# One accumulating bank for both expert groups, output and product in pieces, and a moved weight load, in a fused attention and mixture-of-experts kernel

## Chip, cores and metric

The kernel runs on one core of a Trainium2 chip. The metric is the device time of one execution in microseconds. "The span" is the time from the first to the last instruction in the profiled execution.

## What is computed

Three steps follow one another on 4 x 768 = 3072 tokens of 384 features, all in float32:

```python
x = attn(q, k, v, a_re, a_im)      # scan over time, 32 heads of 48, complex decay
logits = x @ phi                   # 32 slots, 4 for each of 8 experts
d = softmax over tokens (logits);  slot_input = d.T @ x          # 32 x 384
for e in range(8):                 # 4 slots each
    h = maximum(slot_input[e] @ w1[e], 0.0)    # 384 -> 1024
    slot_out[e] = h @ w2[e]                    # 1024 -> 384
x = softmax over slots (logits) @ slot_out     # 3072 x 384
h = x @ w_in;  out = maximum(0.01 * h, h) @ w_out   # 384 -> 2048 -> 384
```

The kernel multiplies slot_out with w_in first (32 slots x 2048, "product"), and only then with the 3072 rows of combine weights.

## The kernel before

A planner (`Plan`, lines 97 to 296) holds every operation with an engine, an estimated cost, what it reads and writes, and a `lead` that raises its priority. It lays all operations out in time by these estimates and then emits them in that order, so each engine's queue is a fixed order. `after` gives the planner an order between two operations and nothing else. Tiles come from tags with a fixed number of buffers; waits follow from the tiles that an instruction touches.

The stages, in order of time: attention in 12 units with the slot sums of `slots`; the experts; the feed-forward part.

*Experts.* The weights w1 and w2 are 64 slabs of 128 x 768 (384 KB): 32 of w1, 32 of w2. `load_slabs` (line 406) issues them on SP through `load` (line 351; all loads carry line 352). Some w2 slabs lie in pairs of half-size buffers (`halved`). The experts are two groups of four; expert g of a group uses column group g of TensorE, 32 output partitions from 32g on. All 32 slots are multiplied with each expert's weights, and the 4 right ones are cut out afterwards.
`layer1(gr)` (line 924) runs once for each group: four steps i of 12 matmuls (L934, two instructions each) into two banks, then ReLU on ACT (L939) or DVE (L941), transposes (L945) and copies of each expert's slots (L952) into h1T, which holds zeros elsewhere. `layer2(gr)` (line 958) adds 32 matmuls (L970) into a bank of its own for each group. `output(gr)` (line 978) scales 384 columns by 1/den on ACT (L982), transposes three blocks (L986) and copies the slots of four experts on DVE (L994) into soT.
siT holds the slot inputs, transposed; DVE writes it (L915).

*Product* (line 1002): for each half j of w_in's columns, 12 matmuls (L1014), a high part on ACT (L1017) and a low part on DVE (L1018), then four selections g, each of two matmuls (L1022, L1023) into bank g, copied to gs by ACT (even g, L1029) or DVE (odd g, L1027).

*Feed-forward.* `ffn1` (line 1036) makes one 128 x 384 block of h for step f and row block j: a matmul (L1039), leaky ReLU on ACT (L1041), its high part on ACT (L1042), its low part on DVE (L1043). `ffn2` adds three matmuls for each row tile (L1056 to L1058). The first double loop runs 16 steps f over j = 0 and 1 and needs w_out of step f as a high and a low part. `conv_wo` (line 465) makes these from 64-bit words: a load, Abs on ACT (L439), four operations on DVE (L440 to L443), a copy on ACT (L471), a subtraction on DVE (L472). Step 0 of these has a lead of 26; the others have none.

`combine_t` makes transposed combine weights; its last copies (L884) read banks of the pool `psa`, whose space the expert stage's banks (`psb`) take over.

*Start.* `load_a` (line 482) loads a_re on SP and a_im of unit 0 on ACT's queue; unit 0 comes in three cuts.

Of the kernel before, what the change touches and what calls it, by code (L numbers as in the profile page):

```python
# [10 lines left out]
F32 = mybir.dt.float32  # L11
# [8 lines left out]
DM = H * D  # L20
# [299 lines left out]
def tile_kernel(  # L320
# [63 lines left out]
    t_dd = Tag(mem, "dd", [P, P], 3)  # L384
# [19 lines left out]
    stream = iter([(l, gr, i, g) for l in range(2) for gr in range(2) for i in range(4) for g in range(4)])  # L404

    def load_slabs(n, homes=None):

        for _ in range(n):
            key = next(stream, None)
            if key is None:  # L410
                return
# [7 lines left out]
            for j, (k, v) in enumerate(slabs[key]):  # L419
                n = W // len(slabs[key])  # L420
                load(k, v, src[:, n * j:n * j + n], P * n * 4)
# [59 lines left out]

    def load_a(u):
        s = st[u]
        for i, nm in enumerate(("re", "im")):
            b = s[nm] = t_w()
            for o, e in cuts(u):
                far = u == 0 and i
                plan.add("ACT" if far else "SP", 0.1, lambda b=b, i=i, o=o, e=e, far=far: (A if far else SY).dma_start(b()[:, o:e], a_in[u, i][:, o:e]), [], [(b, o)], nbytes=P * (e - o) * 4)
# [245 lines left out]
    def slots(c):  # L734
# [4 lines left out]
        b, e, lg = (b_sc if last else b_m)(), t_dd(), t_dd()  # L739
# [21 lines left out]
        b2, dd = (b_sc if last else b_m)(), t_dd()  # L761
# [133 lines left out]
    rd, siT, wb = t_sm([P, 1]), t_dd([P, 3, NSL]), t_kt([P, 4, NSL])  # L895
    dg, mt = t_kt([P, P]), t_sm()
    m = nm[:, NCH:NCH + 1]
    b2 = b_sc()
# [16 lines left out]
    si = dve(0.17, lambda: V.tensor_copy(siT().rearrange("p k s -> p (k s)"), b1()[:, :3 * NSL]), [(b1, k) for k in range(3)], [siT])  # L915
# [6 lines left out]
    pool(0.6, lambda: GP.memset(h1T().rearrange("p k s r g i -> p (k s r g i)"), 0.0), [], [(h1T, r, j, g) for r in range(2) for j in range(2) for g in range(4)])  # L922

    def layer1(gr):
        hb = [bank() for _ in range(2)]
        for i in range(4):
            sl = [slabs[0, gr, i, g][0] for g in range(4)]
            assert all(len(slabs[0, gr, i, g]) == 1 for g in range(4))

            def mm(i=i, sl=sl):  # L930
                for k in range(3):
                    for g in range(4):
                        o = 256 * (i % 2)
# [233 lines left out]
```

## Time and profile before

| | us |
|---|---|
| median of 3 runs | 501.98 (501.07 to 503.56) |
| profiled execution, its own time | 502.35 |
| its span | 500.6 |
| granted TensorE clock, mean | 1.000 |
| busy: TensorE matmul / weight load | 485.2 / 440.0 |
| busy: ScalarE / VectorE / GpSimd | 356.5 / 318.6 / 18.2 |

PE is TensorE's matmul, PEld its weight load, ACT ScalarE, DVE VectorE, POOL GpSimd, SP the engine that issues most loads. Line numbers (L970) are those of the kernel before. Rows give a start and a duration from the start of the span.

### The profile page before, as it was taken

The numbers are of one execution on the slowest core, as the hardware profiler recorded it, in microseconds if no ns is written. First come the engines' busy times: TensorE is split into PE (matmuls) and PEld (weight loads), VectorE is DVE, ScalarE is ACT, GpSimd is POOL, SyncE is SP. The second block draws the span as 40 slices with busy tenths as digits, with TensorE's granted clock in tenths as the row PEclk, the third lists the DMA queues.
The fourth block names the chain that finished last, engine by engine and source line by source line (L and its number), as shares of the span: only waits on it lengthen the run. The fifth ranks groups of instructions, "written<-read, shape, count | busy, mean of one in ns | idle before, by whom it ended". The sixth has DMA issues, their size and how long they took to land.

```text
span 500.6 us, 10447 instructions
## 1 busy us (share of the span) xinstructions
PE 485.2 (97%) x4066; PEld 440.0 (88%) x4066; DVE 318.6 (64%) x669; ACT 356.5 (71%) x684; POOL 18.2 (4%) x37
## 2 busy tenths in 40 slices
PE   8797999999999999999999999999999999999997
PEld 8675779979979988889545999999999999999996
DVE  3767899999999998986535999334500542035300
ACT  7998999999999999944215998079802993079502
POOL 1010002001001000001000000000000000000000
PEclk9999999999999999999999999999999999999999
DMA  8987344465677393599899221011000010010002
GB/s 300 324 196 234 98 129 147 109 192 142 181 221 217 75 260 118 191 323 318 286 395 352 64 64 33 0 48 48 2 0 33 17 48 1 0 48 16 33 1 94
DMA packets 46890, 67.09 MB, mean 134 GB/s; under 512 B 22004, under 2 KB 28132, under 8 KB 46840
## 3 DMA queue, kind: packets, MB, share of 16 engines
q1 hardware_dynamic: 46088, 65.99, 41.4%
q8 instruction: 32, 0.52, 0.4%
q10 hardware_dynamic: 432, 0.39, 0.2%
q0 software_dynamic: 320, 0.03, 0.1%
q14 instruction: 18, 0.15, 0.1%
HBM read 61.59 MB, written 4.81 MB: 133 GB/s over the span
## 4 chain that ended last, share of the span: by engine, by line
PE 70%; DVE 15%; ACT 8%; DMA 5%; issue 1%; SPq 0%; ACTq 0%; DVEq 0%
PE b L1056 13%; PE b L1058 13%; PE b L1057 13%; PE bm L683 5%; PE bsc L658 5%; PE b L1039 4%; PE btr L643 4%; PE bc L562 3%; PE bsc L700 3%; DMA w<-in_w_dram 2%; DVE w L619 2%; DVE sc L661 2%; DMA w<-in_wo_dram 2%; DVE q L628 2%; DVE k L628 1%; PE b L934 1%
## 5 line engine op out<-in xcount | busy, mean ns | idle before, releaser
L1043 DVE TENSOR_TENSOR w<-x,w 128x384 fp32r<-128x384 f32 x128 | 69.0, 555 | 104.6 <-ACT w L1042 103.8
L1056 PE MATMUL b<-w 128*128 128x384 f32 x384 | 128.5, 335 | 0.0
L1058 PE MATMUL b<-w 128*128 128x384 f32 x384 | 128.3, 334 | 0.0
L1057 PE MATMUL b<-w 128*128 128x384 f32 x384 | 128.3, 334 | 0.0
L1056 PEld LDWEIGHTS b<-w 128*128 128x128 f32 x384 | 72.1, 188 | 0.3 <-ACT x L1041 0.2
L1057 PEld LDWEIGHTS b<-w 128*128 128x128 f32 x384 | 72.1, 188 | 0.0
L1058 PEld LDWEIGHTS b<-w 128*128 128x128 f32 x384 | 72.1, 188 | 0.0
L1065 ACT ACTIVATE k<-b 128x384 f32<-128x384 f32 x24 | 11.4, 488 | 79.1 <-PE b L1058 78.9
L1042 ACT ACTIVATE w<-x 128x384 fp32r<-128x384 f32 x128 | 63.4, 525 | 4.9 <-PE b L1058 3.2
L1041 ACT ACTIVATE x<-b 128x384 f32<-128x384 f32 x128 | 59.9, 487 | 2.4 <-PE b L1039 1.5
L658 PE MATMUL bsc<-qt,kt 96*128 96x128 f32 x384 | 50.8, 278 | 0.4 <-DVE S L710 0.2
L658 PEld LDWEIGHTS bsc<-qt,kt 96*128 96x128 f32 x384 | 46.4, 192 | 2.1 <-DVE S L710 0.5
L661 DVE TENSOR_TENSOR sc<-bsc,tri_r 128x512 f32<-128x512 f32 x48 | 32.5, 684 | 7.3 <-PE bsc L658 6.9
L683 PE MATMUL bm<-sc,w 128*64 128x128 f32 (+1 forms) x384 | 35.5, 275 | 0.0
L649 ACT ACTIVATE qt<-btr 96x512 f32<-96x512 f32 x48 | 28.4, 591 | 9.2 <-PE btr L643 9.1
L186 ACT ACT_TABLE_LOAD x25 | 32.1, 1283 | 2.6 <-issue 2.2
L643 PE MATMUL btr<-ident,k 128*96 128x128 f32 x192 | 29.3, 275 | 2.4 <-ACT kt L649 1.7
L683 PE MATMUL bm<-qt,S 96*48 96x128 f32 x320 | 31.1, 272 | 0.0
L700 PEld LDWEIGHTS bsc<-w,k 128*96 128x96 f32 x320 | 28.9, 165 | 2.0 <-issue 1.0
L643 PE MATMUL btr<-ident,q 128*96 128x128 f32 x192 | 29.5, 276 | 1.2 <-DVE kt L647 0.6
L700 PE MATMUL bsc<-w,k 128*96 128x48 f32 x320 | 29.6, 247 | 0.3 <-PE bm L771 0.3
L643 PEld LDWEIGHTS btr<-ident,q 128*96 128x96 f32 x192 | 21.0, 127 | 6.2 <-issue 1.7
(179 smaller groups left out, 798.2 us busy)
## 6 DMA issues: line engine op xcount, KB each, us to landing
w<-in_w_dram SPq DMA_DIRECT2D x50, 384.0 KB, 6.1
w<-in_qkv_dram SPq DMA_DIRECT2D x36, 384.0 KB, 5.9
w<-in_a_dram SPq DMA_DIRECT2D x22, 384.0 KB, 4.2
w<-in_wi_dram SPq DMA_DIRECT2D x16, 384.0 KB, 4.2
w<-in_wo_dram SPq DMA_DIRECT2D x16, 384.0 KB, 5.5
out_dram<-k SPq DMA_DIRECT2D x24, 192.0 KB, 1.9
cs<-in_w_dram SPq DMA_DIRECT2D x4, 384.0 KB
k<-in_w_dram SPq DMA_DIRECT2D x6, 192.0 KB, 3.7
```

The lines of the kernel that those rows point to most:

```text
L186: self.preload(TABLES[name])
L643: T.transpose(b()[:96, P * i:P * i + P], src()[:, i].rearrange("p t d -> p (t d)"), ident)
L658: T.matmul(b()[:, P * i:P * i + P], lhsT=k()[:96, i, :], rhs=q()[:96, i, :], start=True, stop=True)
L661: dve(c_dve(512), lambda: V.tensor_tensor(t(), b().rearrange("p (i t) -> p i t", t=P), tri.unsqueeze(1).to_broadcast([P, 4, P]), op=ALU.mu ...
L683: T.matmul(y()[64 * j:64 * j + m, o:o + P], lhsT=l, rhs=r, start=kind == 0, stop=kind == 1 or c == 0)
L700: T.matmul(b()[:96, D * i:D * i + D], lhsT=ks[i // 4]()[:, i % 4].rearrange("p t d -> p (t d)"), rhs=v()[:, D * g:D * g + D], start=True, ...
L1041: act(NG, lambda: A.activation(u(), b()[:, :NG], AF.Prelu, alpha=0.01), [b], [u])
L1042: act(NG, lambda: A.activation(g()[:, 0], u(), AF.Copy), [u], [(g, 0)])
L1043: dve(c_dve(NG), lambda: V.tensor_tensor(g()[:, 1], u(), g()[:, 0].bitcast(F32), op=ALU.subtract), [u, (g, 0)], [(g, 1)])
L1056: T.matmul(b()[:, :DM], lhsT=lh, rhs=wh()[:, i], start=f == FO[0], stop=False)
L1057: T.matmul(b()[:, :DM], lhsT=ll, rhs=wh()[:, i], start=False, stop=False)
L1058: T.matmul(b()[:, :DM], lhsT=lh, rhs=wl()[:, i], start=False, stop=f == FO[-1])
```

## The change

- The slabs come in the order layer, step, group, expert. `layer1(j)` now covers two steps i of both groups, which add into one bank: siT has 48 columns for each k (16 slots of group 0, 16 zeros, 16 slots of group 1), and each group multiplies with a window of 32, in which the other group's slots are zero. GpSimd clears siT; DVE copies group 0's slots, ACT group 1's. ReLU, transposes and copies run on halves of the bank.
- `layer2()` adds both groups into one bank; `output()` runs once, in three pieces of 128 columns that share the transposes' bank.
- The last four slabs are loaded in halves, the four first halves first, and the last step is split so.
- `product()` waits for one k at a time; the second half has a lead lower by 8; two selections share a bank.
- Step 0 of `conv_wo` loses its lead of 26.
- In the first four units of `ffn1` the high part is written by ACT from the bank.
- In the planned order, unit 1's a_re load comes after unit 0's loads.

```diff
-    stream = iter([(l, gr, i, g) for l in range(2) for gr in range(2) for i in range(4) for g in range(4)])
+    stream = iter([(l, gr, i, g) for l in range(2) for i in range(4) for gr in range(2) for g in range(4)])
...
+        for _, _, k, v, src, n in sorted(later, key=lambda x: x[:2]) if homes is None or together else later:
+            load(k, v, src, P * n * 4)
...
+    def pieces(n):
+
+        out = []
+        for _ in range(n):
+            b = t_w([P, 2, HW])
+            out.append([((b, j), lambda b=b, j=j: b()[:, j]) for j in range(2)])
+        return out
...
+                    [], [(b, o)], nbytes=P * (e - o) * 4, after=[s0[-1]] if u == 1 and not i else [],
...
+    pool(0.3, lambda: GP.memset(siT().rearrange("p k s -> p (k s)"), 0.0), [], [(siT, r) for r in range(2)])
...
-    si = dve(0.17, lambda: V.tensor_copy(siT().rearrange("p k s -> p (k s)"), b1()[:, :3 * NSL]), [(b1, k) for k in range(3)], [siT])
+    own = lambda gr: b1()[:, :3 * NSL].rearrange("p (k r s) -> p k r s", r=2, s=16)[:, :, gr]
+    si = dve(0.15, lambda: V.tensor_copy(siT()[:, :, 0:16], own(0)), [(b1, k) for k in range(3)], [(siT, 0)])
+    act(48, lambda: A.activation(siT()[:, :, 32:48], own(1), AF.Copy), [(b1, k) for k in range(3)], [(siT, 1)])
...
+    def layer1(j):
+        hb = bank()
+        for i in (2 * j, 2 * j + 1):
+            for gr in range(2):
...
+                            T.matmul(
+                                hb()[32 * g:32 * g + 32, o:o + 256], lhsT=siT()[:, k, 16 * gr:16 * gr + NSL],
+                                rhs=sl[g][1]()[:, 256 * k:256 * k + 256], start=k == 0 and gr == 0, stop=k == 2 and gr == 1,
+                            )
+
+                pe(1.3, mm, [(siT, gr)] + [x[0] for x in sl], [hb, (hb, i % 2)])
+        hs, bs = t_kt(), [bank() for _ in range(2)]
+        for n in range(2):
+            x = slice(256 * n, 256 * n + 256)
+            if n:
+                act(256, lambda x=x: A.activation(hs()[:, x], hb()[:, x], AF.Relu), [(hb, n)], [(hs, n)])
+            else:
+                dve(c_dve(256), lambda x=x: V.tensor_scalar(hs()[:, x], hb()[:, x], 0.0, None, op0=ALU.max), [(hb, n)], [(hs, n)])
...
+    def layer2():
+        b = l2[0] = bank()
+        for i in range(4):
+            for gr in range(2):
+                sl = [slabs[1, gr, i, g] for g in range(4)]
+                for js in ((0,), (1,)) if len(sl[0]) > 1 and i == 3 and gr else ((0, 1),):
...
+    def output():
+        b = l2[0]
         plan.lead = 25.0
         so, b2 = t_x(), bank()
...
+        for k in range(3):
+            x = slice(P * k, P * k + P)
+            act(P, lambda x=x: A.activation(so()[:, x], b()[:, x], AF.Copy, scale=rd()), [b, rd], [(so, k)])
+            pe(0.12, lambda k=k, x=x: T.transpose(b2()[:, 160 * k:160 * k + P], so()[:, x], ident), [(so, k)], [(b2, k)])
+            for gr in range(2):
+                own = lambda k=k, gr=gr: b2()[:, 160 * k:160 * k + 144].rearrange("p (g c) -> p g c", c=36)[:, :, 16 * gr:16 * gr + SPE]
+                dve(0.09, lambda k=k, gr=gr, own=own: V.tensor_copy(soT()[:, k, 16 * gr:16 * gr + 16].rearrange("p (g i) -> p g i", i=SPE), own()), [(b2, k)], [(soT, gr, k)])
...
+        N, lead = 256, plan.lead
+        bs, b2 = [bank() for _ in range(2)], {}
         for j in range(2):
             b, y = bs[j], slice(N * j, N * j + N)
+            plan.lead = lead - 8.0 * j
+            for k in range(3):
...
+                pe(0.44, mm, [(soT, r, k) for r in range(2)] + [(wi[2 * g + j], i) for g in range(4) for i in range(2)], [b])
...
+                if g % 2 == 0:
+                    b2[g // 2] = bank()
+                b4, z = b2[g // 2], slice(N * (g % 2), N * (g % 2) + N)
...
+        if j < 2 and f in FO[:ahead]:
+            act(NG, lambda: A.activation(g()[:, 0], b()[:, :NG], AF.Prelu, alpha=0.01), [b], [(g, 0)])
+            act(NG, lambda: A.activation(u(), b()[:, :NG], AF.Prelu, alpha=0.01), [b], [u])
...
-    load_slabs(64)
+    load_slabs(8)
+    load_slabs(4, pieces(4), True)
     select()
...
     for f in FO[:4]:
-        plan.lead = 26.0 if f in FO[:1] else 0.0
+        plan.lead = 0.0
         conv_wo(f)
```

## Rows read from the trace of the kernel before

**Rows 1.** The page, busy time of each engine, share of the span, instructions.
```profile
PE 485.2 (97%) x4066; PEld 440.0 (88%) x4066; DVE 318.6 (64%) x669; ACT 356.5 (71%) x684; POOL 18.2 (4%) x37
```
**Rows 2.** Two stages: length, busy of each engine, clock, DMA share, GB/s.
```profile
249.00:266.00 17.00, 17.00 (x216) 7.57 (x208) 5.21 (x25) 2.28 (x4) 1.04 (x2) 1.00 1.02 392
275.00:287.00 12.00, 12.00 (x70) 11.73 (x69) 11.93 (x28) 12.00 (x31) 0.00 (x0) 1.00 0.24 68
```
**Rows 3.** Timeline of SP's loads: start, duration, what, how many.
```profile
245.48 0.38 SPq L352 DMA_DIRECT2D w<-in_wo_dram  x1
245.96 12.58 SPq L352 DMA_DIRECT2D w<-in_w_dram  x13
259.18 20.61 SPq L352 DMA_DIRECT2D w<-in_wo_dram  x11
```
**Rows 4.** Timeline of TensorE in layer 2; idle time before and its releaser in brackets.
```profile
254.88 1.50 PE L970 MATMUL b<-w,h 128*32 128x384 f32 x16
...
265.24 0.14 PEld L970 LDWEIGHTS b<-w,h 128*32 128x32 f32 x2 [0.46 <-DMA w<-in_w_dram]
266.22 0.16 PEld L970 LDWEIGHTS b<-w,h 128*32 128x32 f32 x8 [0.85 <-DMA w<-in_w_dram]
...
266.22 1.48 PE L970 MATMUL b<-w,h 128*32 128x384 f32 x10 [0.15 <-DMA w<-in_w_dram]
```
**Rows 5.** Timeline from the end of layer 2 to the feed-forward part.
```profile
267.74 0.58 ACT L982 ACTIVATE x<-b,sm 128x384 f32<-128x384 f32 x1
...
268.95 0.40 DVE L994 COPY so<-b 128x12 f32<-128x12 f32 x4
...
269.50 2.80 PE L1014 MATMUL b<-wi,so 128*32 128x256 f32 x48 [0.58 <-DVE so L994]
...
275.32 0.19 PEld L1056 LDWEIGHTS b<-w 128*128 128x128 f32 x1 [0.20 <-ACT x L1041]
```
**Rows 6.** DMA in 236 to 240 us, then in 262 to 268 us.
```profile
DMA packets 801, 1.30 MB, mean 326 GB/s; under 512 B 94, under 2 KB 660, under 8 KB 801
q1 hardware_dynamic: 801, 1.30, 95.5%
...
DMA packets 874, 2.39 MB, mean 398 GB/s; under 512 B 97, under 2 KB 97, under 8 KB 874
q1 hardware_dynamic: 874, 2.39, 103.1%
```
**Rows 7.** Groups by line in 242 to 276 us: busy us, mean ns | idle before.
```profile
L934 PE MATMUL b<-w,dd 128*32 128x256 f32 x192 | 11.0, 380 | 0.4 <-ACT yt L884 0.4
L970 PE MATMUL b<-w,h 128*32 128x384 f32 x72 | 8.4, 489 | 0.2 <-DMA w<-in_w_dram 0.2
...
L945 PE MATMUL b<-ident,kt 128*128 128x128 f32 x16 | 2.6, 285 | 0.0
```
**Rows 8.** Timeline of TensorE, the start of layer 1.
```profile
242.13 1.07 PE L934 MATMUL b<-w,dd 128*32 128x256 f32 x16 [0.41 <-ACT yt L884]
```
**Rows 9.** Lines L764 (idle before it, us, times) and L765: two readers of one bank.
```profile
L764 DVE COPY dd<-bm x5: 279/281/292, 70.5 to 217.0; 128x128 f32<-128x128 f32 x5
  ACT logits L765: 0.3, 1
...
L765 ACT ACTIVATE logits<-bsc x1: 259/259/259, 239.1 to 239.1; 128x128 f32<-128x128 f32 x1
```
**Rows 10.** Timeline: first and last operation of wo's step 0, then of step 2.
```profile
252.25 0.58 ACT L439 ACTIVATE w<-w 128x384 f32<-128x384 f32 x1 [5.23 <-DMA w<-in_wo_dram]
255.39 0.56 DVE L472 TENSOR_TENSOR w<-w 128x384 fp32r<-128x384 f32 x1
...
268.22 0.55 ACT L439 ACTIVATE w<-w 128x384 f32<-128x384 f32 x1
279.65 0.55 DVE L472 TENSOR_TENSOR w<-w 128x384 fp32r<-128x384 f32 x1
```
**Rows 11.** Timeline of ACT at the start: the first reader of unit 1's a_re.
```profile
10.23 0.83 ACT L510 ACTIVATE w<-w 128x768 f32<-128x768 f32 x1
```

More of the change, by code (lines that the diff above doesn't have):

```diff
@@ L479, in cuts @@
         return parts.get(u, [(0, W)])
+    s0 = []
     def load_a(u):
@@ L487, in load_a @@
                 far = u == 0 and i
[L488 removed]
+                ld = plan.add(
+                    "ACT" if far else "SP", 0.1, lambda b=b, i=i, o=o, e=e, far=far: (A if far else SY).dma_start(b()[:, o:e], a_in[u, i][:, o:e]),
+                    [], [(b, o)], nbytes=P * (e - o) * 4, after=[s0[-1]] if u == 1 and not i else [],
+                )
+                if u == 0:
+                    s0.append(ld)
     def load_qkv(u):
@@ L738, in slots @@
         plan.lead = 25.0 if last else 0.0
-        b, e, lg = (b_sc if last else b_m)(), t_dd(), t_dd()
+        b, e, lg = (b_sc if last else b_m)(), t_dd([P, P]), t_dd([P, P])
         ts = [yt[c, i] for i in range(4)]
@@ L921, in tile_kernel @@
     h1T = t_h1()
[L922 to L933, printed above, removed]
-                        T.matmul(hb[i // 2]()[32 * g:32 * g + 32, o:o + 256], lhsT=siT()[:, k, :], rhs=sl[g][1]()[:, 256 * k:256 * k + 256], start=k == 0, stop=k == 2)
-            pe(1.35, mm, [siT] + [x[0] for x in sl], [hb[i // 2]])
-        for j in range(2):
-            b, hs = bank(), t_kt()
-            if j == 0:
-                act(512, lambda hs=hs: A.activation(hs(), hb[0](), AF.Relu), [hb[0]], [hs])
-            else:
-                dve(c_dve(512), lambda hs=hs: V.tensor_scalar(hs(), hb[1](), 0.0, None, op0=ALU.max), [hb[1]], [hs])
-            def tr(hs=hs, b=b):
-                for k in range(4):
-                    T.transpose(b()[:, P * k:P * k + P], hs()[:, P * k:P * k + P], ident)
-            pe(0.44, tr, [hs], [b])
-            for g in range(4):
-                c0 = 36 * g + 16 * gr
-                dve(
-                    0.1,
-                    lambda j=j, b=b, g=g, c0=c0: V.tensor_copy(h1T()[:, 4 * j:4 * j + 4, gr, gr, g, :], b().rearrange("p (k c) -> p k c", c=P)[:, :, c0:c0 + SPE]),
-                    [b], [(h1T, gr, j, g)],
@@ L978, in output, with mm @@
-    def output(gr):
-        b, last = l2[gr][0], l2[1][1]
+            for gr in range(2):
+                sl = [slabs[1, gr, i, g] for g in range(4)]
+                for js in ((0,), (1,)) if len(sl[0]) > 1 and i == 3 and gr else ((0, 1),):
+                    def mm(i=i, gr=gr, sl=sl, js=js):
+                        for j in js:
+                            k = 2 * i + j
+                            for g in range(4):
+                                rhs = sl[g][j][1]() if len(sl[g]) > 1 else sl[g][0][1]()[:, DM * j:DM * j + DM]
+                                T.matmul(
+                                    b()[32 * g:32 * g + 32, :DM], lhsT=h1T()[:, k, gr].rearrange("p r g i -> p (r g i)"),
+                                    rhs=rhs, start=k == 0 and gr == 0, stop=k == FE // P - 1 and gr == 1,
+                                )
+                    pe(0.65 * len(js), mm, [(h1T, i, gr)] + [x[0] for y in sl for j, x in enumerate(y) if len(y) == 1 or j in js], [b])
```

96 lines of the change are left out of this document (41 added, 55 removed).

## The prediction

> **What bounds the kernel now.** I read the page first. TensorE is busy for 97% of the span [rows 1], so the question is not which engine is slow but where TensorE still waits, and what would fill those waits. The stages come next [rows 2]: from 275 us on TensorE is full (12.00 of 12.00, 70 instructions, so 0.171 us each), with DVE (11.93, 28 instructions, 0.43 us each) and ACT full beside it. Work before 275 us therefore counts one for one: whatever brings the first L1056 forward shortens the span, unless DVE or ACT then lag. In 249 to 266 us TensorE also reads as full, but so do the DMA engines (share 1.02, 392 GB/s): each w2 slab arrives there at about the pace at which TensorE eats it, and busy time alone does not say which leads.
>
> The weight loads of TensorE settle it [rows 4]. Layer 2 starts at 254.88; its last matmuls stand still for 0.46 us and 0.85 us for slabs, and the last ten instructions start at 266.22 when the last slab lands, ending at 267.70. So the end of layer 2 is set by DMA. SP's order shows what lies ahead of that slab [rows 3]: the wo load of step 0 is issued at 245.48, in front of 13 slabs; the other wo loads come behind, from 259.18.
>
> From 267.70 a pure chain follows [rows 5]: ACT scales 384 columns (267.74, 0.58), TensorE transposes three blocks, DVE makes four copies (from 268.95), and L1014 starts at 269.50: 1.80 us. Then TensorE runs the product, the selections and six first-layer matmuls almost without a gap, and the first L1056 is loaded at 275.32 after a 0.20 us wait for ACT.
>
> **The change, part by part.** The sum is made against the profiled execution (span 500.6, its own time 502.35, so 1.75 around the span). The median of the runs shown is 501.98, 0.37 below it; I subtract the same microseconds from the median.
>
> *wo load behind the slabs.* 393,216 bytes at 392 GB/s [rows 2] are 1.00 us less in front of the last slab. TensorE's layer 2 could use it: it is waiting there. This moves the last landing from 266.22 to 265.22. The price is that step 0 of wo is converted in the tail, not at 252 to 256 us [rows 10]; see DVE below. SP passes 13 slabs with it, and these gain; nobody else waits on it.
>
> *Last four slabs in halves, first halves first.* After the last landing ten TensorE instructions were left (1.48 us [rows 4]); now two, in one column group. Four of the ten follow one another in one column group, so at 0.49 us for one [rows 7] they come (1.48 - 0.49) / 3 = 0.33 us apart; two take an estimated 0.33 + 0.49 + 0.05 = 0.87 us, 0.61 less. Against it, 192 KB loads move more slowly. In 236 to 240 us, mostly such loads, 326 GB/s at a share of 95.5% passed; in 262 to 268 us whole loads made 398 at 103.1% [rows 6]. The 1.57 MB of four slabs take 4.1 us at the one rate and 4.6 at the other, both scaled to a full share: 0.5 more. The ends are 0 (the queue is full anyway) and 0.9 (raw rates). I take 0.5, because the scaled rates compare like with like. Landing 265.72, end of layer 2 at 266.59: **1.11 us gained**.
>
> *Both groups in the same banks.* Matmul counts stay (192 instructions in layer 1, 11.0 us; 128 in layer 2). Eight of the 16 transposes L945 go, 1.3 of 2.6 us [rows 7], with half of the copies L952, the second scaling, and three of the six transposes L986, which ran beside that scaling. The zero columns cost a POOL memset, on an idle queue, and a second copy of siT on ACT. ACT is idle there, and group 1 needs it only one matmul group (an eighth of 11.0 us) after layer 1's start at 242.13, which was released by the copy L884 [rows 8], not by siT. None of this reaches the end, because layer 2 waits for slabs. But there is a new wait inside layer 1. ReLU of one half of a bank now runs while TensorE should fill the other half. Such pairs are kept apart in this kernel: DVE's copy L764 waited 0.3 us until ACT's L765 was through, although the two read different columns of one bank [rows 9]. So I expect TensorE to stand about 0.5 us (a ReLU at DVE's mean of 0.43 us and the hand-overs) once in each of the two layer-1 passes. 242.13 + 11.0 + 1.3 + 1.0 gives 255.4 for the start of layer 2 and 266.0 for its end without slab waits (32 steps of 0.33), 0.6 us before DMA lets it end. If that cover goes, each further 0.1 us counts. Bounds: 0 to 0.5 us on the path; I take 0.
>
> *Output in 128-column pieces.* If ACT, TensorE and DVE overlapped freely, the first product could start after one ACT piece (0.26 us, the row of L765 [rows 9]), one transpose (0.28 [rows 7]) and two copies (half of the 0.40 [rows 5]) with their hand-overs, 1.0 us after layer 2: 0.8 gained. But the three transposes write one bank, from which DVE copies. Kept apart in the same way [rows 9], each copy then also waits for the transposes put before it, and the third transpose for the first copy. Following that order by hand, the first product starts 1.67 us after layer 2: 0.13 gained. The ends are 0.1 and 0.8. I take **0.3**, because the row is of the very same situation, and because the pieces k=0 and k=1 can still overlap with the product, whose matmuls now wait for one k each.
>
> The Trainium skill, in PSUM — Partial Sum Buffer, section "PSUM bank collisions raise a hardware error", says that two engines must not touch one bank and quadrant at once, whichever columns they use, and that the chip does not arbitrate, so that software must guard by bank. That rule speaks against finer pieces within one bank: by it the gain would be 0.13, by column-wise freedom 0.8. The trace agrees with it as far as it shows one such wait (0.3 us [rows 9]).
>
> *Product and selections.* The same 48 and 16 instructions. Two selections now share a bank that ACT and DVE both read, so that DVE's casts of the odd ones wait some 0.3 us for ACT. DVE has other work to place there. The second half may be put back by 8 us of priority; the work stays.
>
> *First four first-layer units.* ACT writes the high part straight from the bank, without its own earlier result: same instructions, and the **0.20 us** wait before 275.32 [rows 5] should go.
>
> *DVE in the tail.* New there: step 0's conversion. Until step 1 of wo is ready DVE needs 20 operations (ten of conversion, two low parts, four casts, four of the first layer) of 0.43 us and six copies of 0.1: 9.2 us from 267.3, and 0.3 of waits: 276.8. TensorE asks for it at 275.32 - 1.5 + 18 x 0.171 = 276.9. An even race; I add **0.1 us**. The ends are 0 and the rival below.
>
> *load_a.* Unit 1's first load is put behind unit 0's last in the planned order: it may change places with another load on SP, a slot of 1 us. Its reader starts at 10.23 with no wait before it [rows 11]: nothing. A wider dd tile costs no time. Every order is planned anew, though, also before 240 us; from these rows I can only allow for it in the range (0.5 us either way).
>
> Sum: -1.11 - 0.3 - 0.2 + 0.1 = **-1.5 us**: span 499.1, 500.9 for an execution like the profiled one, 500.5 for the median.
>
> **The rivals.**
> *The pieces and halves are worth their full size.* Copies and transposes overlap (0.8), the halves cost nothing (0.5 more) and DVE keeps up: -2.6 to -3. For it: TensorE is otherwise full, so nothing else is late. Against it: such pairs do wait [rows 9], and half loads are slower [rows 6]. Time 499.2.
> *Conversion is late, and the end is slower.* Mechanism: with the wo load behind the slabs, the first L1056 waits for a conversion that shares DVE with the tail. Alone and early, step 0 took from 252.25 to 255.95, 3.7 us; in the busy tail step 2 took from 268.22 to 280.2, 12.0 us [rows 10]. It lands at 266.7. At 3.7 us it is ready at 270.4, 3.4 us before it is asked for (273.8). At 12.0 us it is ready at about 279 and TensorE stands 5.3 us: +3.8, 505.8. It decides from 273.8 on; 1.5 us late eats the gain, 4.0 late makes it slower by 0.5%. If only step 1 is treated like that, it is ready at 279.7, asked for at 276.9: 2.8 late, +1.3, 503.3. Against it: step 2's 12 us were mostly slack, not need.
> *It does not do what it says.* The planner may keep a wo load ahead of some slabs, and halves at the raw rate (0.9) undo the rest: only 0.6 of the remainder is gained, 0.4 to 0.9 is lost, and 0.3 and 0.2 stay: about -0.5, 501.5.
>
> **How the numbers follow.** My forecast, 499.7 to 501.2, has 0.50; full size 0.28; late conversion 0.15 (about half of it beyond 0.5%); no effect of the moved load 0.07. About 0.5%, 2.5 us, is what a measurement of this kernel can tell from no change. Nearly all of the full-size case is beyond it: faster 0.28. Slower by more: 0.07. The rest, 0.65, is within. The range reaches from the full size with the planner's 0.4 us (498.8) to most of step 1's late conversion (502.6).
>
> **What would show it.** Step by step: no wo load among SP's issues before the last slab, and the last w2 landing near 265.7; two, not ten, L970-like instructions behind it; the end of layer 2 near 266.6; the first product matmul 1.0 to 1.7 us later, with DVE and TensorE taking turns on the transposes' bank; the first L1056-like load near 273.8 with no wait for wo; TensorE without gaps from there on. Wrong, if layer 2 ends without waiting for slabs (then TensorE bound it), if the first second-layer matmuls wait for wo conversion, or if the stages before 240 us moved by more than 0.5 us.

## The result and the profile after

The changed kernel takes 508.96 us (median of 508.21 to 510.64) against 502.77 (501.07 to 504.11): ratio 1.013, interval 1.0085 to 1.0174. Repeated later beside other kernels it took 508.32 against 503.21: 1.0112, 1.0086 to 1.0138. It is 5 to 6 us slower, where 1.5 us less was forecast. The profiled execution took 508.21 (span 506.5), 5.9 more than that of before.

The page's busy times hardly move (columns as in [rows 1]): TensorE and ACT are within 0.5 us of before, DVE 0.6 lower. The 5.9 us are waiting time or slower work, and the page hints at two places: TensorE's 22nd and 23rd digits (266 to 291 us) are 8 where before had 9, and PEclk has an 8 in the fourth slice (38 to 51 us).

```profile
PE 485.6 (96%) x4055; PEld 440.1 (87%) x4055; DVE 318.0 (63%) x659; ACT 356.0 (70%) x686; POOL 18.8 (4%) x38
...
PE   8788999999999999999998899999999999999997
...
PEclk9998999999999999999999999999999999999999
```

TensorE's timeline gives the stages. Each row is start, duration, line, tiles and count; in brackets the idle time ahead of it and what ended it.

```profile
244.86 4.09 PE L956 MATMUL b<-w,dd 128*32 128x256 f32 x72 [0.40 <-PE bc L840]
249.55 0.44 PE L973 MATMUL b<-ident,kt 128*128 128x128 f32 x2 [0.60 <-DVE kt L968]
256.91 0.44 PE L973 MATMUL b<-ident,kt 128*128 128x128 f32 x2 [0.65 <-DVE kt L968]
...
265.24 4.36 PE L999 MATMUL b<-w,h 128*32 128x384 f32 x50
270.17 0.59 PE L1013 MATMUL b<-ident,x 128*128 128x128 f32 x2 [0.57 <-ACT x L1012]
271.12 0.30 PE L1013 MATMUL b<-ident,x 128*128 128x128 f32 x1 [0.36 <-ACT w L450]
271.69 2.80 PE L1033 MATMUL b<-wi,so 128*32 128x256 f32 x48 [0.27 <-DVE so L1016]
...
280.00 0.44 PE L1082 MATMUL b<-w 128*128 128x384 f32 x1 [2.12 <-ACT w L482]
...
281.22 0.44 PE L1084 MATMUL b<-w 128*128 128x384 f32 x1 [0.59 <-DVE w L483]
```

Read beside [rows 8, 4, 5]: layer 1 starts 2.73 us later than before, although the change touches no attention code. From there to the end of layer 2 (269.61) it takes 24.74 us instead of 25.57, and the 50 matmuls at the end have no slab wait. The product then comes 2.08 us later instead of 1.80. The first second-layer matmul comes 8.32 us behind the product's first, instead of 5.82, after 2.12 us of standing for a copy of wo. The second layer itself takes 0.90 us more. Together: 2.73 - 0.83 + 0.28 + 2.50 + 0.90 = 5.58, and 5.59 is where its last matmul stands. SP did what the change says: 21 slabs, then wo.

```profile
246.35 18.52 SPq L352 DMA_DIRECT2D w<-in_w_dram  x21
265.09 21.49 SPq L352 DMA_DIRECT2D w<-in_wo_dram  x12
```

**The clock.** A part of the 2.73 is no work of the change. Windows of the changed kernel (length; busy time of PE, PEld, DVE, ACT, POOL with counts; granted clock; DMA share; GB/s), where TensorE resumes after a wait of 2.1 us:

```profile
39.00:40.00 1.00, 0.85 (x2) 0.49 (x3) 1.00 (x3) 0.10 (x1) 0.00 (x0) 1.00 1.05 421
40.00:41.00 1.00, 1.00 (x5) 0.66 (x4) 0.85 (x2) 0.00 (x0) 0.00 (x0) 0.67 1.02 398
41.00:42.00 1.00, 1.00 (x7) 0.98 (x6) 0.00 (x0) 0.22 (x1) 0.00 (x0) 0.50 0.84 214
42.00:43.00 1.00, 1.00 (x7) 0.97 (x6) 0.00 (x0) 1.00 (x2) 0.00 (x0) 0.50 1.06 90
43.00:44.00 1.00, 1.00 (x6) 0.74 (x4) 0.86 (x1) 0.80 (x2) 0.00 (x0) 0.62 0.84 269
```

The same microseconds of the kernel before, after a wait of 2.19 us:

```profile
40.00:41.00 1.00, 1.00 (x7) 0.71 (x6) 0.85 (x2) 0.00 (x0) 0.00 (x0) 1.00 1.04 411
41.00:42.00 1.00, 1.00 (x11) 0.89 (x10) 0.00 (x0) 0.76 (x2) 0.00 (x0) 1.00 0.85 229
```

The clock falls to 0.50, the lower of its levels (1.2 instead of 2.4 GHz), for some 3 us: here called the dip. Each run lists its mean granted clock, and the counts below take 0.999 and 1.000 as runs without the dip. The mean tells how much low clock a run had, not where: the profiled run of a_ord_lead stands at 0.998 without a low stretch before its last matmul, and some kernels have a second low stretch near 280 us (below). The kernel before, timed beside the experiments, stands at 0.999 or 1.000 in 37 of 101 runs (median 501.70) and at 0.993 to 0.998 in the other 64 (503.36). The dip costs about 1.7 us and falls on the kernel before too. Its profiled execution happened to be without; all ten runs of the changed kernel (median 508.5) stand at 0.992 to 0.997, and its two profiled ones have the dip at 40 us. Runs with the dip against runs with the dip, the change costs 5.1 us. But the changed kernel's runs stand lower, at 0.994 on average against 0.996. At equal mean clock the change costs 4.7 us at 0.997 (508.13, two runs, against 503.45, 36 runs), 5.4 at 0.995 (three runs against six) and 4.7 at 0.993 (four against seven).

### The profile page after: what moved, and what is told of

The parts are those of the page before. It is cut to its first block, busy times and chain, and to the rows that moved or that the text cites. A ratio compares the mean times of both kernels' runs of the same rounds, so it can differ in the third digit from the quotient of the medians.

```text
span 506.5 us, 10429 instructions
## 1 busy us (share of the span) xinstructions
PE 485.6 (96%) x4055; PEld 440.1 (87%) x4055; DVE 318.0 (63%) x659; ACT 356.0 (70%) x686; POOL 18.8 (4%) x38
## 4 chain that ended last, share of the span: by engine, by line
PE 75%; ACT 13%; DVE 7%; DMA 2%; issue 2%; SPq 0%; ACTq 0%; DVEq 0%
PE b L1084 13%; PE b L1083 13%; PE b L1082 13%; PE bm L701 6%; PE btr L661 5%; PE bsc L676 5%; PE b L1061 4%; PE bc L580 3%; PE bsc L718 3%; ACT L186 2%; PE b L956 2%; PE b L999 2%; ACT qt L667 1%; PE bm L743 1%; DMA w<-in_wi_dram 1%
## 5 line engine op out<-in xcount | busy, mean ns | idle before, releaser
L1068 ACT ACTIVATE w<-x 128x384 fp32r<-128x384 f32 x124 | 62.2, 526 | 5.0 <-PE b L1084 3.2
L1067 ACT ACTIVATE x<-b 128x384 f32<-128x384 f32 x124 | 58.8, 489 | 4.1 <-PE b L1061 3.2
```

Source lines behind the costliest of these rows:

```text
L1067: act(NG, lambda: A.activation(u(), b()[:, :NG], AF.Prelu, alpha=0.01), [b], [u])
L1068: act(NG, lambda: A.activation(g()[:, 0], u(), AF.Copy), [u], [(g, 0)])
```

## Experiments

In the table: median, ratio to the kernel before beside it with its interval; medians of the runs without and with the dip (count); and from the profiled execution's TensorE timeline, in us: start of layer 1, from there to the end of layer 2, to the product, to the second layer, and the second layer's length.

| kernel | us | ratio | no dip | dip | layer 1 at | layers | output | product | second layer |
|---|---|---|---|---|---|---|---|---|---|
| before | | | 501.70 (37) | 503.36 (64) | 242.13 | 25.57 | 1.80 | 5.82 | 221.84 |
| after | 508.96 | 1.0130 (1.0085-1.0174) | (0) | 508.47 (10) | 244.86 | 24.74 | 2.08 | 8.32 | 222.74 |
| after_again | 508.32 | 1.0112 (1.0086-1.0138) | in the row above | | 244.72 | 24.74 | 2.08 | 8.32 | 222.75 |
| a_ord | 504.38 | 1.0033 (1.0012-1.0054) | 503.66 (5) | 505.48 (5) | 243.51 | 24.29 | 2.08 | 6.04 | 224.12 |
| b_ord | 504.48 | 1.0043 (1.0022-1.0064) | 503.96 (5) | 505.87 (4) | 243.95 | 27.06 | 1.80 | 5.85 | 221.86 |
| a_lead | 505.48 | 1.0061 (1.0039-1.0083) | 505.06 (1) | 505.74 (3) | 244.24 | 26.13 | 1.97 | 6.04 | 221.92 |
| a_split | 505.74 | 1.0068 (1.0042-1.0095) | 504.82 (1) | 505.96 (3) | 245.73 | 25.05 | 1.97 | 6.03 | 222.79 |
| a_ord_lead | 504.64 | 1.0035 (1.0016-1.0055) | 503.45 (3) | 504.89 (9) | 241.47 | 26.13 | 2.04 | 6.04 | 223.69 |
| a_ord_split | 504.06 | 1.0019 (0.9997-1.0040) | 502.68 (5) | 504.41 (7) | 241.32 | 24.29 | 2.08 | 6.04 | 223.48 |
| b_lead0 | 502.07 | 0.9987 (0.9967-1.0007) | 501.58 (7) | 503.25 (5) | 241.99 | 24.10 | 1.81 | 6.23 | 222.25 |
| b_split | 502.02 | 0.9994 (0.9976-1.0012) | 501.86 (5) | 502.67 (7) | 241.61 | 24.01 | 1.83 | 6.20 | 222.20 |
| a_best | 507.82 | 1.0102 (1.0074-1.0130) | (0) | 507.82 (6) | 244.22 | 24.29 | 2.08 | 6.71 | 226.37 |
| a_best_nohalf | 506.64 | 1.0073 (1.0048-1.0098) | 503.89 (1) | 506.64 (7) | 242.47 | 24.75 | 1.68 | 6.06 | 226.04 |
| a_best_banks | 507.12 | 1.0094 (1.0064-1.0124) | (0) | 507.12 (6) | 242.12 | 24.30 | 1.34 | 6.69 | 227.29 |
| a_mend | 503.79 | 1.0021 (1.0003-1.0039) | 502.46 (5) | 504.14 (7) | 241.02 | 24.77 | 1.34 | 6.04 | 223.39 |
| a_mend_att | 505.72 | 1.0061 (1.0038-1.0084) | 504.15 (1) | 505.82 (6) | 245.14 | 24.74 | 1.34 | 6.02 | 223.40 |
| b_aft | 503.91 | 1.0017 (0.9996-1.0039) | 501.38 (2) | 504.07 (10) | 243.54 | 26.09 | 1.80 | 5.84 | 221.86 |
| a_noafter | 509.36 | 1.0112 (1.0090-1.0135) | (0) | 509.36 (6) | 244.92 | 24.76 | 2.06 | 8.32 | 224.26 |

**The order of the attention.** The kernel's planner computes one order for all operations. Compared operation by operation, ACT's order differs from before from its 74th operation on, DVE's from the 70th, TensorE's from the 152nd, long before the experts. Neither the swapped loads nor the lost lead of wo, put alone into the kernel before, moves an operation of these three engines there, so it comes from the rest of the change, mostly the rebuilt expert stages; which part of it does it was not tested. Two kernels hold the first 1269 operations (the attention and what leads into the experts) to the other kernel's order: a_ord is the changed kernel in the order of before, b_ord the reverse.

```diff
+FIXED = { "PE": "0 1 1 ...", "ACT": "...", ... }   # the other kernel's order, per engine
                 for o in c:
+                    if o.i in held_to and fixed[e][0] != o.i:
+                        continue
```

> The changed kernel, with the operations up to the start of the expert stage held, on each engine, to the order that they have in the kernel before; all the rest is planned as in the changed kernel. Theory: of the 5.9 us lost, 2.7 are there before the first expert matmul, because the planner, given other work behind, reordered ACT and DVE in attention units 2 to 6 (and the TensorE clock fell once near 40 us). Then layer 1 starts at 242 us instead of 244.9 and the time falls by about 2.7, to 506.3. Rival: the late start comes from the moved loads or from the clock and not from the order of ACT and DVE; then less than 1 us comes back: 508 to 509.

> The kernel before, with the operations up to the start of the expert stage held to the order that they have in the changed kernel (its swap of two first loads is part of that order). Theory of the order: layer 1 starts near 244.9 us instead of 242.1, and the time rises by 2.7, to about 505.4. Rival: the order costs nothing by itself: 502.8, layer 1 at 242.

a_ord gained 3.9 to 4.6 us on the changed kernel (3.0 between their runs with the dip), more than the 2.7 that the order could give, though layer 1 started at 243.51 in its trace, which has the dip, and not at 242. b_ord lost 1.6 of the 2.7 expected. Neither is clean. In a_ord most of the wait for wo went too (product column 6.04), with step 0's lead still lost, and its second layer takes 2.28 us more than before's. In b_ord TensorE stood 1.48 us in the layers for a ReLU that ACT did late, which is no part of the change: of the 2.3 us (runs without the dip) and 2.5 us (with it) that b_ord costs, the layers take 1.49, so 0.8 to 1.0 is left for the order of the attention. The pair a_mend and a_mend_att, below, gives the term by itself.

**The early start of wo.** a_lead gives step 0 of the wo loop its lead back, load and arithmetic; a_split its arithmetic alone, with the load behind the slabs.

```diff
     for f in FO[:4]:
-        plan.lead = 0.0
+        plan.lead = 26.0 if f in FO[:1] else 0.0
```

> The changed kernel, with step 0 of the wo conversion given back its lead of 26, the load too. Theory: the other loss is that step 0's conversion, without its lead, stands in ACT's queue behind the first-layer operations, so that the first second-layer matmul comes 2.5 us and its third 0.6 us late, and steps 1 to 3 lag behind it. Then 2.5 to 3.2 us come back: 505.8 to 506.5. The load stands before the last slabs again, 1.0 us; TensorE does not wait for slabs in the changed kernel, so this costs 0 to 1. Rival: DVE has too little time for the tail in any order, and the wait only moves to a later step: 508 to 509.

> The changed kernel, with the lead of 26 for the arithmetic of wo's step 0 alone; its load stays behind the slabs. Theory: it is the place in ACT's and DVE's queues, not the later load, that makes the conversion late: ready about 5 us earlier, with the first second-layer matmul near 277.6, and 2.0 to 3.0 us back: 506 to 507. Rival: the load behind the slabs lands too late for any priority: then nearly nothing comes back, 508 to 509, and a_lead alone is better.

Both take 2.5 to 3.5 us back (505.48, 505.74): the product column falls from 8.32 to 6.04 and the second layer starts without a wait. The second layer itself is back at 221.92 in a_lead alone; in a_split it stays at 222.79, with a wait of 0.53 us for ACT in it. In a_lead the load stands in front of 17 slabs again, and the layers column shows its price: 26.13 against 24.3 to 25.1 in the rebuilt kernels that have it behind. Its last weight loads wait for slabs, four times 0.27 to 0.38 us. What a_lead took away is seen in the changed kernel's queues, ACT's and, last row, DVE's:

```profile
276.10 0.49 ACT L1064 ACTIVATE w<-b 128x384 fp32r<-128x384 f32 x1
276.49 0.49 ACT L1065 ACTIVATE x<-b 128x384 f32<-128x384 f32 x1
...
278.72 0.56 ACT L1065 ACTIVATE x<-b 128x384 f32<-128x384 f32 x1
279.09 0.47 ACT L1051 ACTIVATE qt<-b 128x256 fp32r<-128x256 f32 x1
279.35 1.01 ACT L482 ACTIVATE w<-w 128x384 fp32r<-128x384 f32 x2
...
274.12 0.55 DVE L454 SCALAR_TENSOR_TENSOR w<-w 128x384 int32<-128x384 int32 x1
```

DVE has the rounded value of step 0 at 274.67. ACT's copy of it starts at 279.35, because eight first-layer operations and a cast stand ahead of it in ACT's queue, back to back from 276.10. In b_lead0, below, the same copy starts at 269.74, 1.84 us behind the first product matmul and ahead of all of them; here it is 7.66 us.

```profile
269.74 0.52 ACT L471 ACTIVATE w<-w 128x384 fp32r<-128x384 f32 x1
...
272.08 0.49 ACT L1041 ACTIVATE x<-b 128x384 f32<-128x384 f32 x1
```

**Is the dip the change's?**

> The changed kernel once more, for its clock. In the first batch the kernel before had a mean granted clock of 0.999 or 1.000 in 8 of its 18 runs (median 502.1 us) and 0.993 to 0.997 in the other 10 (503.5 us); the four runs of the changed kernel seen so far all stood at 0.992 to 0.997. Theory 1: the dip of the clock at 38 to 44 us falls on any kernel of this family by chance and is no work of the change; then some of these runs stand at 0.999 or 1.000 and lie about 1.4 us below the others, near 507.3, and the ratio stays near 1.012. Theory 2: the change brings the dip; then no run reaches 0.999 and the times stay at 508.2 to 510.6.

No run without the dip, so theory 1's number was missed. The edit that reaches that stretch is the swapped start of unit 1's loads; b_aft adds it to the kernel before alone, a_noafter takes it from the changed kernel alone.

```diff
-    [], [(b, o)], nbytes=P * (e - o) * 4, after=[s0[-1]] if u == 1 and not i else [],
+    [], [(b, o)], nbytes=P * (e - o) * 4, after=[],
```

> The kernel before with one edit of the change alone: the first load of unit 1 waits for the last of unit 0, which swaps the start of two loads; the order on every other engine is that of the kernel before. Theory 1 (the dip is chance, the swap is worth nothing): ratio 1.000, dips in some 6 of 10 runs. Theory 2 (the swap brings the dip): dips in every run, about 0.6 us above the kernel before, ratio 1.001.

> The changed kernel without that swap, all else as in it. Theory 1: 508.4 us as the changed kernel, and the dip where that has it. Theory 2: runs without the dip appear, at about 506.8, and the median falls by about 0.6.

Without the swap the changed kernel has the dip in all 6 runs and is no better; with it the kernel before has it in 10 of 12, beside 11 of 17 without, and also shows runs without (500.75, 502.01). The swap is not needed for the dip and does not force it. Kernels with the changed attention order reach a clock of 0.999 or more as well (b_ord in five runs of nine, a_lead, a_split and a_mend_att in one each), so the order doesn't force the dip either. Whether the change makes it likelier (10 of 10 runs against 64 of 101) stays open; the changed kernel's wait of 2.12 us for wo is a second place where the clock can fall, and the mean does not tell the two apart.

a_noafter's trace has a second dip, behind the wait for wo (windows of 2 us, columns as above):

```profile
278.00:280.00 2.00, 0.00 (x0) 0.00 (x0) 2.00 (x6) 2.00 (x7) 0.00 (x0) 1.00 0.12 48
280.00:282.00 2.00, 1.33 (x4) 1.01 (x5) 2.00 (x5) 2.00 (x6) 0.00 (x0) 0.80 0.52 146
282.00:284.00 2.00, 2.00 (x7) 2.00 (x7) 2.00 (x6) 1.69 (x5) 0.00 (x0) 0.50 0.14 55
284.00:286.00 2.00, 2.00 (x11) 2.00 (x11) 1.31 (x4) 0.99 (x3) 0.00 (x0) 0.85 0.00 0
```

Its second layer took 224.26 us, 1.5 more than the changed kernel's in a trace without this dip: a wait of two microseconds can cost nearly as much again.

**The load's place alone, and the order held.** b_lead0 is the kernel before with step 0's lead set to 0: one part of the change alone. a_ord_lead and a_ord_split are a_ord with the lead edits of a_lead and a_split.

```diff
-        plan.lead = 26.0 if f in FO[:1] else 0.0
+        plan.lead = 0.0
```

> The kernel before with one edit of the change alone: step 0 of the wo loop loses its early start, so its load goes behind the last slab and its arithmetic behind the first-layer operations. The order of the attention is that of the kernel before. By the forecast: 0.5 us faster, since layer 2 waits for slabs and the copies have 5.8 us of product to hide behind, ratio 0.999. Theory 1 (the copies of step 0 stand behind the first-layer operations in the queue of ScalarE): the first second-layer matmul waits 2 to 3 us for a copy, ratio 1.004 to 1.006.

> The changed kernel with the first 1269 operations held to the order of the kernel before on each engine, and with the early start of step 0 of the wo loop (load and arithmetic) given back. Theory 1 (the rebuilt expert stages are about 1 us faster, and the loss lies in the order of the attention and in the late conversion): without the dip the product ended 1.0 us ahead of the kernel before in the run that held the order alone, the second layer then lost 2.5 us by late copies; with the copies early nothing is lost and the time is 1.0 us under the kernel before, ratio 0.998. Theory 2 (the second layer loses its time to something else than the copies, since the pieces of the product move it): as with the order alone, 504.4, ratio 1.003.

> As the run before, but only the arithmetic of step 0 starts early; its load stays behind the slabs, as the change has it. Theory 1, with the forecast that a load out from between the slabs gives them 0.5 us: 0.5 us under the run before, ratio 0.997. Theory 2 (layer 2 of the rebuilt stages no longer waits for slabs, so the load's place is worth nothing, and a load that lands late makes the early arithmetic late): level with the run before or up to 1 us above it, ratio 0.998 to 1.000.

Theory 1 fell for b_lead0: no wait for a copy, 24.10 us for the layers instead of 25.57, and 0.41 of it given back on the way to the second layer and 0.41 in it. Losing the lead alone does not make the copy late; that takes the order of the rebuilt stages as well. b_lead0's start of layer 1 and the last row of its layer 2, which ends at 266.09:

```profile
241.99 5.39 PE L934 MATMUL b<-w,dd 128*32 128x256 f32 x96 [0.42 <-ACT yt L884]
...
264.52 1.57 PE L970 MATMUL b<-w,h 128*32 128x384 f32 x16
```

a_ord_lead (1.0035) came out as its theory 2 says. a_ord_split is 0.6 us under it, about the 0.5 of its theory 1, but its ratio of 1.0019 lies 2.5 us above that theory's 0.997. It shows the rebuilt stages at their best, 24.29, and 1.84 us quicker than a_ord_lead's 26.13; but its second layer takes 1.64 us more than before. Its waits between 320 and 480 us name a new one, on TensorE's weight loads:

```profile
PEld b L1117 <- ACT x L1123: 0.9, 5, 0.2
```

Five times the first layer's next matmul waits for ACT to leave a bank (us in total, times, longest). The kernel before has no such line there. The second layer also obeys an order made anew; these waits are about half of the 1.64, and the rest is not accounted for.

**Mending the rest.** b_split is the kernel before with the load behind the slabs and the arithmetic early (a_split's edit). a_best is a_ord_split with the second layer in a_lead's order, a_best_nohalf the same without halves, a_best_banks the same with three banks for the transposes.

```diff
-    load_slabs(4, pieces(4), True)
+    load_slabs(4)
-        so, b2 = t_x(), bank()
+        so, bs = t_x(), [bank() for _ in range(3)]
         for k in range(3):
+            b2 = bs[k]
```

> The kernel before with one edit: the load of wo step 0 goes behind the last slab, its arithmetic keeps its early start. Theory 1 (the load's place is worth about 1.5 us to layer 2 and is the only gain in the change; only the late arithmetic cost 0.8 us of it, when this edit was made without the early start): layer 2 ends 1.5 us earlier against the start of layer 1 (24.1 us instead of 25.57), the second layer starts as far behind the product as before (5.8 us from the product's first matmul), ratio 0.997 and under both kernels. Theory 2 (the arithmetic waits for the later load whatever its start): no better than without the early start, ratio 0.9987.

> The changed kernel with the attention held to the order of the kernel before, the early start of step 0's arithmetic, and the second layer held to an order in which it took 221.9 us. Theory 1 (the rebuilt expert stages themselves gain nothing beside the moved load: 24.3 us from the start of layer 1 to the end of layer 2, where the kernel before with only the load moved took 24.1, and 2.08 us from there to the product, where it took 1.81): 0.5 us slower than the kernel before with only the load and its arithmetic parted, ratio 0.998. Theory 2 (with everything put right the rebuilt stages give the forecast in full): 1.5 us under the kernel before, ratio 0.997, and not above that run.

> As the run before with the last four slabs loaded whole. By the forecast the halves shorten what is left after the last landing by 0.61 us and cost 0.5 in rate: layer 2 ends up to 0.6 us later without them, or 0.1. By theory 1 TensorE waits for no slab in the rebuilt layer 2 (it ends in a row of matmuls without a gap): the end of layer 2 against the start of layer 1 stays at 24.3 us within 0.1, and the time is the same.

> As the second run of this batch with the three transposes of the output in three banks of their own instead of one. Theory 1 (the third transpose waits until DVE has copied the first piece out of the shared bank, although the row names an ScalarE conversion): its wait of 0.36 us goes, and the product starts 1.7 us behind layer 2 instead of 2.08. Theory 2 (it waits for ScalarE, as the row says): the wait stays and the product starts 2.08 us behind layer 2. Between the two times of the whole kernel at most 0.4 us.

b_split has the expected 24.01 us, yet the whole is not told apart from before (0.9976 to 1.0012): 6.20 us to the second layer instead of 5.82, and 0.36 more in it, take half of it back. a_best missed: a_lead's order was made for a load that lands early, and with a late one the second layer stands 2.71 us for a DVE result. In a_best_banks it is 2.71 as well, in a_best_nohalf 2.49. All three traces also have the clock at 0.50 near that wait, for 3.4 us in the first two and 6.8 in a_best_banks (276.19 to 283.02), so that the second layer column holds the wait and the clock. Windows of a_best_banks, columns as above:

```profile
276.00:278.00 2.00, 0.41 (x1) 0.41 (x2) 2.00 (x7) 1.86 (x5) 0.00 (x0) 0.55 0.02 9
278.00:280.00 2.00, 2.00 (x8) 2.00 (x8) 2.00 (x6) 1.02 (x3) 0.00 (x0) 0.50 0.00 0
280.00:282.00 2.00, 2.00 (x8) 2.00 (x8) 2.00 (x5) 1.15 (x3) 0.00 (x0) 0.50 0.26 41
```

That spoils the totals of these three but not their stages. Without halves the layers take 24.75, against both expectations: 0.46 more than in a_best, of which 0.33 is the first wait for a ReLU (0.62 instead of 0.29). They take as long with halves where the same ReLU waits of 0.6 us stand (a_mend 24.77), and TensorE waits for no slab in either: the halves are worth nothing here. With three banks, the transposes run together and the product follows layer 2 by 1.34 us:

```profile
266.98 0.84 PE L1101 MATMUL b<-ident,x 128*128 128x128 f32 x3 [0.57 <-ACT x L1100]
267.75 2.80 PE L1121 MATMUL b<-wi,so 128*32 128x256 f32 x48
```

In the changed kernel the third transpose started at 271.12. The row names an ACT conversion (L450), but ACT's third piece was done at 270.63; what ended just before was DVE's first copy out of that bank, 270.80 + 0.17:

```profile
269.75 0.88 ACT L1012 ACTIVATE x<-b,sm 128x128 f32<-128x128 f32 x3 [9.23 <-PE b L999]
270.52 1.17 ACT L450 ACTIVATE w<-w 128x384 f32<-128x384 f32 x2
270.80 0.17 DVE L1016 COPY so<-b 128x16 f32<-128x16 f32 x1 [8.16 <-PE b L1013]
271.46 0.50 DVE L1016 COPY so<-b 128x16 f32<-128x16 f32 x5 [0.48 <-PE b L1013]
```

**Everything mended, and the attention order by itself.** a_mend is a_best_banks with the second layer in b_split's order; a_mend_att is a_mend with the attention held to the changed kernel's order instead of that of before.

```diff
-FIXED = [attention of before, second layer of a_lead]
+FIXED = [attention of before, second layer of b_split]    # a_mend
+FIXED = [attention of after, second layer of b_split]     # a_mend_att
```

> The changed kernel with the attention held to the order of the kernel before, the three transposes in three banks, the early start of step 0's arithmetic, and the second layer held to the order that the kernel before took with its wo load behind the slabs. Theory 1 (all that was lost lay in order, and the moved load and the pieces in banks of their own are worth 1.3 and 0.5 us by the traces, of which the second layer gives back 0.8): the product ends 1.7 us earlier against the start of layer 1 than in the kernel before, the whole is 1.0 us faster, ratio 0.998, and level with the kernel before with only the load parted from its arithmetic. Theory 2 (the rebuilt stages make the second layer late whatever its order): second layer 223 us or more, ratio 1.003 or above.

> The run before with the attention in the order of the changed kernel, nothing else altered. By the traces (start of layer 1 at 243.95 to 245.73 us in runs with that order and the dip of the clock, 243.51 in the run with the order of the kernel before and the dip): 0.4 to 2.2 us slower than the run before, most likely 1.2, ratio 1.000 to 1.001. Rival (the order costs nothing and the traces differ by the luck of small transfers): level with the run before.

a_mend is 0.2% slower than before (1.0003 to 1.0039): its second layer takes 223.39, as theory 2 says, though the ratio of 1.003 was not reached. TensorE still waits, 1.27 us for DVE's low part of the first layer. This is put down to step 0's conversion, which starts late and stands in DVE's queue with it. a_mend's rows, then b_split's:

```profile
265.94 0.88 ACT L1100 ACTIVATE x<-b,sm 128x128 f32<-128x128 f32 x3 [9.20 <-PE b L1086]
266.70 1.01 ACT L536 ACTIVATE w<-w 128x384 f32<-128x384 f32 x2
...
274.88 0.44 PE L1171 MATMUL b<-w 128*128 128x384 f32 x1 [1.27 <-DVE w L1157]
```

```profile
264.39 0.58 ACT L983 ACTIVATE x<-b,sm 128x384 f32<-128x384 f32 x1 [11.37 <-PE b L971]
265.01 0.58 ACT L439 ACTIVATE w<-w 128x384 f32<-128x384 f32 x1
```

Its first conversion (L536) starts behind the scaling of both groups, 0.91 us behind the end of layer 2 (265.79). In b_split it stands between the two groups' scalings (L439 at 265.01), 0.60 us ahead of layer 2's end: the rebuilt stages have no first group that ends early and leaves such a gap.

a_mend_att is 1.7 us slower than a_mend, in the runs with the dip (505.82 and 504.14) as in those without (504.15, a single run, and 502.46). That is the price of the order of the attention in this pair. More traces give 1.4: with the dip, layer 1 starts at 243.95 to 245.73 us in seven traces with the changed order (mean 244.79) and at 242.47 to 244.22 in four with that of before (243.44). With b_ord's 0.8 to 1.0 the price is 0.8 to 1.7 us. a_mend_att's trace has TensorE waits that a_mend's lacks, such as these for an ACT copy of qt:

```profile
66.08 0.64 PE L748 MATMUL btr<-ident,q 128*96 128x128 f32 x4 [0.25 <-ACT qt L754]
69.80 0.64 PE L748 MATMUL btr<-ident,q 128*96 128x128 f32 x4 [0.55 <-ACT qt L754]
```

## Why the prediction was wrong

Two steps failed most. Losing step 0's lead was priced at 0.1 us by a race on DVE; its copies stood in ACT's queue, and giving the lead back brought 2.28 us ahead of the second layer and 0.82 in it (a_lead). The new order of everything was allowed 0.5 us either way; in the attention alone it cost 0.8 to 1.7.

At equal mean clock the change costs 4.7 to 5.4 us. The order of the attention is 0.8 to 1.7 of them (1.7 by a_mend_att against a_mend). By the changed kernel's trace the way to the second layer costs 2.50 and the second layer 0.90, the output 0.28, and the layers give 0.83 back: 2.85. Together 3.7 to 4.6. The other 0.1 to 1.8 has no measurement of its own. The terms are not independent either: a_ord, with nothing but the order of the attention put back, lost most of the wait for the copies too.

*What bounds the kernel: right.* Layer 2 waited for slabs, and the wo load in front of them was the reason. Moved alone, it brought 1.47 us (b_lead0) and 1.56 (b_split), more than the 1.00 taken from its bytes, and nearer to the two waits of [rows 4], 0.46 + 0.85 = 1.31, neither of which is in b_lead0's or b_split's layers. That term was too small.

*Last slabs in halves:* 0.11 net was forecast, nothing was found.

*Both groups in the same banks: "none of this reaches the end" was wrong.* With the load behind the slabs, the rebuilt layers take 24.3 to 25.1 us and the old ones 24.0 to 24.1: the rebuild costs 0.2 to 1.0. Two waits for a ReLU, forecast at 0.5 each, came (0.60 and 0.65 in the changed kernel), though what stands there is the transposes that need its result (L973) and not the matmuls into the other half of the bank, so that these rows do not show the bank's guard at work. The step that failed is that a wait for slabs would cover them. Once layer 2 stops waiting for slabs TensorE is the bound, as the prediction's own list of what would make it wrong says, and then every such wait counts.

*Output pieces: wrong sign.* The order worked out by hand, third transpose behind the first copy, is what happened. It gave 1.67 us, and where DVE happened to be busy when the first transpose was done, so that all three ran ahead of the copies, it took 1.68 (a_best_nohalf); in the changed kernel it took 2.08. The mistake was to take 0.3 between that hand order and column-wise freedom. With a bank for each piece the gain would have been 0.46 (1.80 to 1.34). The rule of the Trainium skill that the prediction weighed (PSUM — Partial Sum Buffer, section "PSUM bank collisions raise a hardware error": guard by bank, whichever columns are used) fits this: 0.74 us lies between one bank and three. The wait ends behind another engine's copy and is gone with three banks, so it is put down to the program's own guard of the bank.

*ACT's wait of 0.20 and DVE's 0.1:* the first went, but its place was taken by 2.12 us, and the step that failed is how step 0's copies were hidden. The rival "conversion is late" had the place right: the first L1056. It looked for the delay on DVE, which had its value 4.7 us before ACT's copy began; the queue that mattered was ACT's, where eight first-layer operations stood in front. Costing an edit at nothing needs the in-order queue that stands ahead of each of its instructions, not only the busy share.

*"Every order is planned anew ... 0.5 us either way":* 0.8 to 1.7 us in the attention. This allowance was a guess without a row behind it, and it is the largest single error next to the copies. The swapped loads of load_a, priced at nothing, agree with b_aft and a_noafter, neither of which is told apart from its own base.

*The rest of the working.* The clock was not in it: the changed kernel's runs stand at a lower mean clock than those of before, which is 0.2 to 0.9 of the 5.6 us between the median of its ten runs (508.47) and that of the 101 (502.87). The chance of a slower kernel, 0.07, came from summing terms as if the order stayed: a_best_banks and a_mend, the same instructions with the second layer in two orders, lie 3.3 us apart, by a wait of 2.71 us instead of 1.27 and a clock that stands low for 6.8 us in one trace and not in the other.

No version tried is shown to beat the kernel before: b_lead0 and b_split are 0.1% under it, which their intervals do not tell from none.

## What to carry to other kernels

Where one planner orders everything, an edit at the end moves instructions at the start: compare the orders engine by engine before pricing the edit, and price what moved. When a load is taken from in front of the work, follow its arithmetic through each in-order queue to the instruction that waits for it; what it gained there it can lose here. Pieces that write one bank are no pieces while another engine reads that bank.

## What the runs showed of the hardware

- After TensorE stood for some 2 us, traces of nearly the same program went on at 1.00 in one and at 0.50 for about 3 us in another; by the mean clocks 64 of 101 runs of one kernel had it, at 1.7 us each. By the Trainium skill (TensorE: Matmul & The Clock Gate, Part 1) the chip's watch on TensorE runs freely and isn't reset when a kernel starts, so that one kernel differs from run to run; these runs agree in that one kernel's runs differ.
- Seven kernels with the attention in the order of before, and without the dip, started layer 1 at 241.02 to 242.13 us. What sets this was not tested; one such difference can be followed, at a chain of 3 KB transfers among large loads. In two kernels with the same order, the changed one and a_lead, SP issues the same write at 107.77 and at 106.18, because it waits 3.2 us for its GpSimd operand in one and 1.4 in the other; the wi load issued behind it is then waited for by ACT in one and not in the other. The changed kernel's rows, then a_lead's:

```profile
107.77 0.33 SPq L601 DMA_DIRECT2D dr<-cr  x1
...
114.24 0.56 ACT L450 ACTIVATE w<-w 128x384 f32<-128x384 f32 x1 [1.54 <-DMA w<-in_wi_dram]
```

```profile
106.18 0.58 SPq L601 DMA_DIRECT2D dr<-cr  x1
...
112.73 0.55 ACT L450 ACTIVATE w<-w 128x384 f32<-128x384 f32 x1
```
